# Linear attention and a feed-forward layer in one kernel: one batch's value loads behind a transpose, and another order of matmul products

## The chip, the cores and the metric

The kernel runs on one core of a Trainium2 chip. The core has a matrix engine (TensorE, shown as PE, its weight loads as PEld), a vector engine (VectorE, DVE), an activation engine (ScalarE, ACT), a general engine (GpSimd, POOL) and a queue engine that only issues transfers (SyncE, SP). Each takes its instructions in program order and waits on semaphores. Transfers are issued from SP, from POOL or from ACT and are carried out by 16 DMA engines that all of them share. TensorE reads from the on-chip memory SBUF and writes its results to eight PSUM banks[...].

The metric is the time of one execution on the device, in microseconds (us). Below about half a per cent a change of this kernel can't be told from none.

## The reference

There are 8 batches, 8 heads, 576 rows and 64 columns for each of q, k and v, in float32. The first part is attention with two separate softmaxes and no score matrix, the second a normalised feed-forward layer of width 2048 on 512 columns:

```python
q_s = softmax(q over the columns)          # per row
k_s = softmax(k over the rows)             # per column
kv  = einsum('bhsd,bhse->bhde', k_s, v)    # 64 x 64 per head
att = einsum('bhsd,bhde->bhse', q_s, kv)
x   = att with the heads side by side      # 8 x 576 x 512
xn  = (x - mean) / sqrt(var + 1e-6) * g_ln
out = x + relu(xn @ w_ch1) @ w_ch2
```

## The kernel before

**Tiling.** Each batch gives one chunk of 512 rows (chunks 0 to 7); the 64 rows left over in each of the 8 batches form a ninth chunk, called C9 in the code. A chunk's rows are held as four tiles t = 0 to 3 of 128 rows. All matrix work is in bfloat16.

**A chunk's attention.** `exp_q` and `exp_k` (ACT, lines 208 and 173) take the exponentials. `eq_T` (line 240) transposes the exponentials of q with one DMA from SP (line 236) into a tile `eqT`. `kv_mm` (line 275) multiplies k by v, with v taken from the tile `vm`; DVE scales the result into `kv_sb`. `po_mm` (line 313) multiplies `eqT` by `kv_sb`, and `x_fast` (line 372) turns the result into rows `x` and centred rows `xn`. `xn_T` (line 243) transposes `xn` by DMA into `xnT`, two tiles a time. For the ninth chunk, `x_rest` and `xn_out` stand in for `x_fast`.

**A chunk's feed-forward.** The first matmul, from chunk 2 on, is `mm1_fast` (line 581). It mixes plain column blocks (`plain m`), half blocks (`part`) and a Strassen-Winograd scheme with seven products P1 to P7 for each of two groups. The order of these pieces is a list of tokens in `plan`: `x` builds the differences of xnT (tile `ts`, line 561), `C` copies P1's bank as the start of P2 (ACT, line 605), `E` builds the start of P3 (DVE, line 639), `L` finishes one quarter (DVE, line 645). The second matmul, `mm2_fast` (line 804), uses seven products of 16 matmuls; line 722 issues them all and line 706 makes the sums `hs` that they need. For the ninth chunk it is `last_products` (line 753), in the order 1, 5, 2, 6, 7, 3, 4, and its rows leave in small stores on SP and ACT (line 773). There `seed_c` copies product 1's bank as the start of product 2, `copy_u("s2")` copies the bank after product 6 (line 748), and `seed_e` adds it to product 5's bank as the start of product 3.

**What sets the order.** Every engine's order is the program order. `run` (line 885) walks a chunk's matmul steps, each with a weight in units (a 128x512 matmul is one unit, half a one half), and before each step emits the side work whose due time in units has passed. A chunk is 60 units of first matmul and 56 of second. The side work of chunk c prepares chunks c+1 and c+2. All due times of chunks 2 to 7 stand in `plan`; those of chunk 1 stand in `second_side` (line 967).

**The loads in question.** `load_batch` (line 1157) loads q and k of a batch from SP and v in eight DMAs of 64 KB from POOL (line 1168); the DMA changes float32 to bfloat16 on the way and writes pieces of 64 columns into `vm`. In chunk 1's side work batch 3's q is loaded at unit 8, its k at unit 31 and its v at unit 40, while `eq_T(2)`, which chunk 2's attention needs within the same chunk, is due at unit 14.2. The outputs of each chunk go out from POOL (lines 494 and 740), so they are queued behind v's loads.

```python
s += [(10, lambda: exp_q(2, 0, 4)), (14, lambda: exp_q(2, 2, 4)), (14.2, lambda: eq_T(2))]
s += [(p, lambda w=w: load_batch(3, (w,))) for p, w in ((8, 2), (31, 0), (40, 1))]
```

The plan's entries that matter: `order` and `o9` are the token orders of chunks 2 to 7 and of the ninth; `xT` and `rT` place the transposes of xn; `prep` places exp_q, eq_T, the left-over rows and exp_k of the batch after next; `qw1` places four sums of the first weights, needed from chunk 2 on; `s9` places four sums of the ninth chunk; `rest` places the ninth chunk's attention in chunk 7.

Of the kernel before, what the change touches and what calls it, by code (L numbers as in the profile page):

```python
# [21 lines left out]
def kernel(  # L22
# [16 lines left out]
    nc = tc.nc  # L39
# [5 lines left out]
    T = 4  # L45
# [4 lines left out]
    NP = H // 2  # L50
# [6 lines left out]
    NG = 2  # L57
    M0 = KO2 - 4 * NG
    plan = dict(
        order=('P1 0|x 0|C 0|part 0|part 2|P2 0|P5 0|x 1|P6 0|E 0|plain 3|P7 0|plain 2|P3 0|P1 1|C 1|P4 0|L 0|plain 5|P6 1|P5 1|P2 1|plain 4|E 1|P7 1|plain 6|plain 7|P4 1|L 1|P3 1').split('|'),  # L60
        red=[9.5, 19.0, 21.0, 26.5, 35.5],
        kv=[6.0, 26.0],
        po=[[37.5, 42.5], [45.0, 48], [56, 67.5], [84.5, 90.0]],
        sq=[47, 62.5, 85.0, 109.0],
        xT=[58.0, 98.5, 110.5],
        prep=[62, 80.0, 92.5, 95.0, 97.5, 112.5],
        sum=60,
        qw1=[40, 53, 59.0, 79.0],
        o9=('x 0|x 1|P1 0|C 0|plain 3|part 0|P2 0|P6 0|plain 6|plain 4|P5 0|plain 2|plain 5|P7 0|part 2|P1 1|E 0|C 1|P4 0|L 0|P3 0|P5 1|P6 1|E 1|plain 7|P7 1|P3 1|L 1|P2 1|P4 1').split('|'),
        s9=[54.5, 58.0, 58.0, 58.5],  # L70
        rest=[[23.5, 28.0, 38.0, 51.0], [34.0, 50.5, 61.5, 65.0], [47.0, 63.0, 74.0, 80.0], [62.0, 87.0, 90.0, 92.0]],
        rT=[85.5, 115.0, 120.0],
    )
    T0 = 6
    P0 = S // T0
# [26 lines left out]
    gate = const.tile([P, 4], FP32)  # L102
# [68 lines left out]
    eks, eqs, eqTs, xs, xnTs, rstds = {}, {}, {}, {}, {}, {}  # L171
# [68 lines left out]
    def eq_T(c):  # L240
        dma_T(eqTs[c], eqs[c][0].rearrange("p t h d -> p (t h d)"), 0, T)
# [282 lines left out]
    def quarter_w2(i, g):  # L524

        ks = slice(4 * g, 4 * g + 4)
        rows = [w2_sb[:, 8 * g + odd : 8 * g + 8 : 2, :] for odd in range(2)]
        (b11, b12), (b21, b22) = [(r[:, :, 0:DH2], r[:, :, DH2:DM]) for r in rows]
        t1, t2, t3, t4 = [w2_q[:, n, ks, :] for n in range(4)]
        dst, x, y = ((t1, b12, b11), (t3, b22, b12), (t2, b22, t1), (t4, b21, t2))[i]  # L530
        nc.vector.tensor_sub(out=dst, in0=x, in1=y)
# [163 lines left out]
    def sum_h(g, i):  # L695

        if g == 0 and i == 0:
            hbox["s"] = mlp.tile([P, 4, KH, 2 * P], BF16, tag="hs", name="hs", bufs=1)
        ks = slice(KH // 2 * g, KH // 2 * g + KH // 2)
        s1, s2, s3, s4 = [hbox["s"][:, n, ks] for n in range(4)]  # L700
        a11, a12, a21, a22 = [h_part(odd, half, ks) for half in range(2) for odd in range(2)]
        dst, x, y, op = (
            (s1, a21, a22, ALU.add), (s2, s1, a11, ALU.subtract),
            (s3, a11, a21, ALU.subtract), (s4, a12, s2, ALU.subtract),
        )[i]
        nc.vector.tensor_tensor(out=dst, in0=x, in1=y, op=op)  # L706
# [18 lines left out]
    def bank(name):  # L725
        slot = {"a": 4, "c": 5, "b": 1, "e": 3, "d": 0}[name]
        hbox[name] = bank_of([P, 2, DH2], FP32, "b" + name, slot)
# [18 lines left out]
    def copy_u(name):  # L746
        hbox[name] = mlp.tile([P, 2, DH2], FP32, tag=name, name=name, bufs=1)
        nc.scalar.copy(hbox[name], hbox["a"])  # L748

    def add_u(dst, src):  # L750
        nc.vector.tensor_tensor(out=hbox[dst], in0=hbox["b"], in1=hbox[src], op=ALU.add)

    def last_products(product):

        c = C9
        yl = raw.tile([P, T, DM], FP32, tag="qt", name="yl")

        def part(t, col):
            return yl[:, t, DH2 * col : DH2 * col + DH2]

        def stt(t, col, src, add=None):
            cols = slice(DH2 * col, DH2 * col + DH2)
            nc.vector.scalar_tensor_tensor(
                part(t, col), in0=src, scalar=rstds[c][:, t : t + 1],
                in1=xs[c][0][:, t, cols] if add is None else add, op0=ALU.mult, op1=ALU.add,
            )

        def store(t0, tn, col):
            cols = slice(DH2 * col, DH2 * col + DH2)
            for half, eng in enumerate((nc.sync, nc.scalar)):  # L770
                ps = slice(64 * half, 64 * half + 64)
                to = out[2 * t0 + half : 2 * (t0 + tn) - 1 + half : 2, SM:S, cols]
                eng.dma_start(to.transpose([1, 0, 2]), yl[ps, t0 : t0 + tn, cols])

        def both(name, t0, col, add=False):
            for t in range(2):
                stt(t0 + t, col, hbox[name][:, t], part(t0 + t, col) if add else None)

        def own_bank():
            bank("d")  # L780

        def seed_e():
            bank("e")
            add_u("e", "s2")

        def seed_c():
            bank("c")
            nc.scalar.copy(hbox["c"], hbox["a"])

        product(1, "a", first=True, at={  # L790
            0: [lambda: sum_h(1, 0), lambda: sum_h(1, 1), lambda: sum_h(1, 2), lambda: sum_h(1, 3)],
            15: [seed_c]})
        product(5, "b", first=True)
        product(2, "c", at={15: [lambda: both("c", 0, 0), lambda: store(0, 2, 0)]})
        product(6, "a", at={15: [lambda: copy_u("s2"), seed_e]})
        product(7, "a", at={0: [lambda: both("b", 2, 1)], 15: [
            lambda: both("a", 2, 1, True), lambda: stt(3, 0, hbox["a"][:, 1]),
            lambda: store(2, 2, 1)]})
        product(3, "e", at={15: [lambda: both("e", 0, 1), lambda: store(0, 2, 1), own_bank]})
        product(4, "a", ts=(0,), at={7: [lambda: stt(2, 0, hbox["a"][:, 0]), lambda: store(2, 1, 0)]})  # L800
        product(4, "d", ts=(1,), own=True, at={
            15: [lambda: stt(3, 0, hbox["d"][:, 1], part(3, 0)), lambda: store(3, 1, 0)]})
# [164 lines left out]
    def second_side():  # L967

        s = [(p, lambda i=i: quarter_w2(i, 1)) for i, p in enumerate((1, 4, 44, 46))]
        s += [(8.0, lambda: xn_pT(1, 3, nc.scalar))]  # L970
        s += [(10, lambda: exp_q(2, 0, 4)), (14, lambda: exp_q(2, 2, 4)), (14.2, lambda: eq_T(2))]
        s += [(p, lambda i=i: quarter_w1(i)) for i, p in enumerate(plan["qw1"])]
        s += [(42, lambda: square_sum(1, 2)), (50, lambda: square_sum(1, 3)), (71, lambda: rstd_op(1))]
        s += [(p, lambda w=w: load_batch(3, (w,))) for p, w in ((8, 2), (31, 0), (40, 1))]
        s += [(100, lambda: load_batch(4, (2,)))]
        s += [(p + 15, fn) for p, fn in sums_fast(2)]
        s += [(18, lambda: exp_k(2, 0, 4)), (22, lambda: exp_k(2, 2, 4)), (26, lambda: prep_kvrem(2))]
        s += [
            (p, lambda j=j, e=e: cast_v(2, j, e))
            for p, j, e in ((31, 0, None), (31.4, 1, None), (31.8, 2, None), (32.2, 3, None))  # L980
        ]
        s += spread(
            [lambda j=j, t=t: kv_mm(2, j, t) for j in range(NP) for t in range(T + 1)], 43, 53
        )
        s += [(53, lambda: start_x(2))]
        for t, (p0, p1) in enumerate(((55, 58), (64, 67), (75, 80), (87, 93))):
            s += spread([lambda t=t, i=i: po_mm(2, t, i) for i in range(NP)], p0, p1)
            s += [(p1, lambda t=t: x_fast(2, t)), ((73, 82, 92, 105)[t], lambda t=t: square_sum(2, t))]
        s += [(78, lambda: xn_T(2, 0, 2)), (98, lambda: xn_T(2, 2, 2)), (106, lambda: rstd_op(2))]
        s += [(75, lambda: exp_q(3, 0, 4)), (79, lambda: exp_q(3, 2, 4)), (85, lambda: eq_T(3))]  # L990
        s += [(97, lambda: exp_k(3, 0, 4)), (108, lambda: exp_k(3, 2, 4)), (113, lambda: prep_kvrem(3))]
        return s
# [37 lines left out]
    def xn_pT(c, t, eng):  # L1030
        pe_T(xnTs[c], xs[c][2][:, t], t, eng)
# [125 lines left out]
    def load_batch(b, parts=(2, 0, 1)):  # L1157

        alloc(b, parts)
        for which in parts:  # L1160
            if which != 1:
                nc.vector.memset(raws[b][which][0:1, 0, 0, 0:1], 0.0)
        for which in parts:
            if which != 1:
                load_main(nc.sync, b, which, 0, H)
                continue
            for h in range(H):
                nc.gpsimd.dma_start(  # L1168
                    vm[:, b % 2, :, h // 2, 64 * (h % 2) : 64 * (h % 2) + 64],
                    v[b, h, 0:SM, :].rearrange("(p t) d -> p t d", t=T),  # L1170
                )
        if 1 in parts:
            load_kvrem(nc.sync, b)
# [114 lines left out]
```

## Time and profile before

Seven runs gave a median of 283.59 us, between 282.07 and 285.1. The profiled execution took 282.14 us, of which the profile's span is 280.4; 1.7 us lie outside the span.

| where | span, us | TensorE busy, us | VectorE busy, us | ScalarE busy, us |
|---|---|---|---|---|
| start to chunk 0's first matmuls | 0 to 34.0 | 32.54 | 19.59 | 22.09 |
| chunk 0's second matmul, chunk 1's first rows | 34.0 to 62.0 | 27.71 | 22.06 | 18.48 |
| rest of chunk 1 | 62.0 to 85.5 | 19.69 | 16.95 | 14.51 |
| chunk 2 | 85.5 to 112.7 | 27.20 | 22.64 | 21.11 |
| chunk 3 (4, 5 and 6 are alike) | 112.7 to 140.0 | 27.30 | 22.67 | 20.64 |
| chunk 7 | 221.9 to 249.0 | 27.10 | 23.96 | 18.63 |
| ninth chunk, with the last stores | 249.0 to 280.4 | 25.89 | 16.02 | 12.09 |

Each row is one stretch of the span. How to read it: an engine that is busy all the time can only be helped by fewer or faster instructions; one with gaps can be helped by whatever ends the gap. TensorE has its gaps in three places: the beginning, the rest of chunk 1, and the ninth chunk.

### The profile page before, as it was taken

The numbers are of one execution on the slowest core, as the hardware profiler recorded it, in microseconds if no ns is written. First come the engines' busy times: TensorE is split into PE (matmuls) and PEld (weight loads), VectorE is DVE, ScalarE is ACT, GpSimd is POOL, SyncE is SP. The second block draws the span as 40 slices with busy tenths as digits, with TensorE's granted clock in tenths as the row PEclk, the third lists the DMA queues.
The fourth block names the chain that finished last, engine by engine and source line by source line (L and its number), as shares of the span: only waits on it lengthen the run. The fifth ranks groups of instructions, "written<-read, shape, count | busy, mean of one in ns | idle before, by whom it ended". The sixth has DMA issues, their size and how long they took to land.

```text
span 280.4 us, 6073 instructions
## 1 busy us (share of the span) xinstructions
PE 269.3 (96%) x2362; PEld 214.2 (76%) x2365; DVE 213.0 (76%) x492; ACT 186.7 (67%) x365; POOL 66.8 (24%) x104
## 2 busy tenths in 40 slices
PE   8999999994999999999999999999999999999993
PEld 6888856762788688868986988698779877887673
DVE  4673778683988897889788978797879979982853
ACT  4568862793577888587868776877786489557500
POOL 3931224560007400820181018102000300030000
PEclk9999999999799999999999999999999999999999
DMA  7999999999489997799499948954920910160014
GB/s 189 243 207 206 335 212 331 230 243 214 76 148 297 247 204 111 227 233 168 89 288 232 128 105 264 127 86 106 244 42 8 204 57 0 37 182 9 2 37 112
DMA packets 84767, 45.41 MB, mean 162 GB/s; under 512 B 61442, under 2 KB 81410, under 8 KB 84739
## 3 DMA queue, kind: packets, MB, share of 16 engines
q0 software_dynamic: 32272, 22.09, 42.0%
q1 hardware_dynamic: 51874, 22.42, 38.7%
q10 hardware_dynamic: 592, 0.52, 0.6%
q8 instruction: 18, 0.29, 0.4%
q14 instruction: 11, 0.08, 0.1%
HBM read 36.70 MB, written 9.44 MB: 165 GB/s over the span
## 4 chain that ended last, share of the span: by engine, by line
PE 88%; DMA 4%; DVE 4%; ACT 2%; issue 0%; DVEq 0%
PE ba L722 19%; PE q L578 15%; PE ph L457 14%; PE ph L472 9%; PE bc L722 5%; PE be L722 5%; PE bb L722 5%; PE pc L517 4%; DMA eqT<-eq 4%; PE warm L903 3%; PE pkv L288 3%; PE po L322 3%; DVE hs L706 1%; PE ptr L1012 1%; ACT eq L212 1%; PE po L329 1%
## 5 line engine op out<-in xcount | busy, mean ns | idle before, releaser
L722 PEld LDWEIGHTS <-hs 128*128 128x128 bf16 x512 | 49.8, 98 | 7.2 <-issue 0.9
L457 PE MATMUL ph<-xnT,w_sb 128*128 128x512 bf16 x200 | 54.0, 385 | 0.0
L740 POOL DMA_DIRECT2D out_dram<-ot x28 | 15.2, 548 | 140.4 <-DVE ot L734 140.4
L447 ACT ACTIVATE hT<-ph 128x512 bf16<-128x512 f32 x50 | 29.9, 605 | 16.5 <-PE ph L457 15.4
L722 PEld LDWEIGHTS <-hT 128*128 128x128 bf16 x384 | 36.3, 99 | 4.7 <-ACT hT L598 0.3
L472 PE MATMUL ph<-xnT,w_sb 128*128 128x256 bf16 (+1 forms) x320 | 37.1, 267 | 0.0
L1168 POOL DMA_DIRECT2D vm<-in_v_dram x40 | 29.6, 745 | 11.1 <-DMA out_dram<-ot 6.1
L457 PEld LDWEIGHTS <-w_sb 128*128 128x128 bf16 x200 | 19.7, 99 | 15.9 <-issue 0.8
L472 PEld LDWEIGHTS <-w_sb 128*128 128x128 bf16 x320 | 29.1, 98 | 3.1
L722 PE MATMUL ba<-w_q,hs 128*128 128x256 bf16 x256 | 30.7, 273 | 0.7 <-ACT s L748 0.7
L322 PE MATMUL po<-kv_sb,eqT 128*128 128x128 bf16 x128 | 24.3, 222 | 4.0 <-DMA eqT<-eq 3.8
L375 DVE SCALAR_TENSOR_TENSOR x<-po,rq 128x512 bf16<-128x512 f32 x30 | 20.6, 686 | 9.2 <-PE po L322 9.0
L598 ACT ACTIVATE hT<-q 128x512 bf16<-128x512 f32 x42 | 24.1, 597 | 2.8 <-PE q L578 2.6
L228 DVE TENSOR_REDUCE zq<-eq 128x8 f32<-128x512 bf16 x32 | 20.9, 680 | 6.2 <-ACT eq L212 3.5
L578 PE MATMUL q<-ts,w_q 128*128 128x256 bf16 x168 | 25.7, 273 | 0.0
L482 ACT ACTIVATE hT<-ph 128x512 bf16<-128x512 f32 x34 | 20.3, 601 | 7.3 <-PE ph L472 7.1
L578 PEld LDWEIGHTS <-w_q 128*128 128x128 bf16 x224 | 19.8, 98 | 6.1 <-issue 0.3
L706 DVE TENSOR_TENSOR hs<-hT 128x1024 bf16<-128x1024 bf16 x32 | 21.3, 688 | 3.2 <-ACT hT L447 1.6
L748 ACT COPY s<-ba 128x512 f32<-128x512 f32 x15 | 8.8, 585 | 20.7 <-PE ba L722 20.6
L288 PE MATMUL pkv<-vm,ek 128*128 128x129 bf16 x112 | 21.2, 220 | 0.0
L650 ACT COPY s<-q 128x512 f32<-128x512 f32 x28 | 16.3, 582 | 2.5 <-PE q L578 2.4
L322 PEld LDWEIGHTS <-eqT 128*128 128x128 bf16 x128 | 11.9, 99 | 7.8 <-DMA eqT<-eq 4.3
(145 smaller groups left out, 509.0 us busy)
## 6 DMA issues: line engine op xcount, KB each, us to landing
out_dram<-ot POOLq DMA_DIRECT2D x32, 256.0 KB, 3.7
qt<-in_q_dram SPq DMA_DIRECT2D x5, 1024.0 KB, 10.9
kt<-in_k_dram SPq DMA_DIRECT2D x5, 1024.0 KB, 9.0
w_sb<-in_moe_w_ch_dram POOLq DMA_DIRECT2D x8, 512.0 KB, 14.2
vm<-in_v_dram POOLq DMA_DIRECT2D x40, 64.0 KB, 9.2
qt<-in_q_dram POOLq DMA_DIRECT2D x2, 1024.0 KB, 15.8
kt<-in_k_dram POOLq DMA_DIRECT2D x2, 1024.0 KB, 16.2
kt<-in_k_dram SPq DMA_DIRECT2D x4, 288.0 KB, 5.8
```

The source lines that it names most:

```text
L228: nc.vector.reduce_sum(eqs[c][1][:, t], eqs[c][0][:, t], axis=AX.X)
L288: nc.tensor.matmul(pkv[:, j % 2, 0:w], lhsT, rhs, start=(t == 0 and j % 2 == 0), stop=(t == last), skip_group_check=True,)
L322: nc.tensor.matmul(pobox["p"][:, i * P : i * P + P], eqTs[c][:, t, i, :], kv_sb[:, c, i, :], start=True, stop=True,)
L375: nc.vector.scalar_tensor_tensor(x[:, t].rearrange("p (h d) -> p h d", h=H), in0=pobox[c, t].rearrange("p (h d) -> p h d", h=H), scalar=1. ...
L447: nc.scalar.activation(dst, src, AF.Relu)
L457: nc.tensor.matmul(hbox["ph"], w1_sb[:, ko, m * P : (m + 1) * P], xnTs[c][:, :, ko, :], start=(ko == 0), stop=(ko == KO1 - 1),)
L472: nc.tensor.matmul(ph[:, m % 2, at : at + tn], w1_sb[:, ko, m * P : (m + 1) * P], xnTs[c][:, t0 : t0 + tn, ko, :], start=(m % 2 == 0 and a ...
L578: nc.tensor.matmul(hbox["q", slot][:, m], lhsT, rhs, start=first and i == 0, stop=ko == 1, skip_group_check=True)
L598: nc.scalar.activation(hbox["h"][:, m0 : m0 + 2, 2 * nh : 2 * nh + 2], hbox["q", slot].rearrange("p m (t c) -> p m t c", t=2), AF.Relu,)
L706: nc.vector.tensor_tensor(out=dst, in0=x, in1=y, op=op)
L722: nc.tensor.matmul(hbox[bank][:, t], lhsT, rhs, start=first and (own or t == 0) and k == 0, stop=k == KH - 1, skip_group_check=True)
L1168: nc.gpsimd.dma_start(vm[:, b % 2, :, h // 2, 64 * (h % 2) : 64 * (h % 2) + 64], v[b, h, 0:SM, :].rearrange("(p t) d -> p t d", t=T),)
```

## The change

It holds batch 3's v loads: POOL first copies a few values of `eqT` of batch 2, so everything behind that copy on POOL waits until that transpose has landed. It changes the token orders of the first matmul, moves due times of side work in chunks 1 to 7, and in the ninth chunk's second matmul puts product 6 ahead of product 2, with product 5's rows taken out at product 2's first step. The computation is the same; one small copy on POOL is added.

```diff
-        order=('P1 0|x 0|C 0|part 0|part 2|P2 0|P5 0|x 1|P6 0|E 0|plain 3|P7 0|plain 2|P3 0|P1 1|C 1|P4 0|L 0|plain 5|P6 1|P5 1|P2 1|plain 4|E 1|P7 1|plain 6|plain 7|P4 1|L 1|P3 1').split('|'),
+        order=('x 0|P1 0|C 0|part 0|P2 0|part 2|P5 0|x 1|P6 0|E 0|plain 3|P7 0|plain 2|L 0|P3 0|P1 1|C 1|P4 0|plain 5|P6 1|plain 4|P5 1|P2 1|P7 1|E 1|plain 7|plain 6|L 1|P4 1|P3 1').split('|'),
-        xT=[58.0, 98.5, 110.5],
-        prep=[62, 80.0, 92.5, 95.0, 97.5, 112.5],
+        xT=[60.5, 123.5, 110.5],
+        prep=[68, 71.0, 86.0, 90.5, 101.5, 113.5],
-        qw1=[40, 53, 59.0, 79.0],
-        o9=('x 0|x 1|P1 0|C 0|plain 3|part 0|P2 0|P6 0|plain 6|plain 4|P5 0|plain 2|plain 5|P7 0|part 2|P1 1|E 0|C 1|P4 0|L 0|P3 0|P5 1|P6 1|E 1|plain 7|P7 1|P3 1|L 1|P2 1|P4 1').split('|'),
-        s9=[54.5, 58.0, 58.0, 58.5],
-        rest=[[23.5, 28.0, 38.0, 51.0], [34.0, 50.5, 61.5, 65.0], [47.0, 63.0, 74.0, 80.0], [62.0, 87.0, 90.0, 92.0]],
-        rT=[85.5, 115.0, 120.0],
+        qw1=[47.5, 51.5, 55.0, 63.0],
+        o9=('P1 0|C 0|plain 5|plain 4|P2 0|x 0|plain 2|plain 3|part 0|P6 0|part 2|P5 0|x 1|P7 0|E 0|P1 1|C 1|plain 6|P3 0|plain 7|L 0|P6 1|P4 0|P5 1|E 1|P7 1|P2 1|L 1|P4 1|P3 1').split('|'),
+        s9=[47, 52.5, 52.5, 57.5],
+        rest=[[12.5, 29.5, 39.5, 49.5], [27.5, 35.5, 64.5, 73.0], [45.5, 60.0, 72.5, 73.5], [61.5, 67.0, 73.5, 91.0]],
+        rT=[83.5, 129.5, 91.0],
...
-        product(2, "c", at={15: [lambda: both("c", 0, 0), lambda: store(0, 2, 0)]})
         product(6, "a", at={15: [lambda: copy_u("s2"), seed_e]})
-        product(7, "a", at={0: [lambda: both("b", 2, 1)], 15: [
+        product(2, "c", at={0: [lambda: both("b", 2, 1)], 15: [lambda: both("c", 0, 0), lambda: store(0, 2, 0)]})
+        product(7, "a", at={15: [
...
-        s += [(p, lambda w=w: load_batch(3, (w,))) for p, w in ((8, 2), (31, 0), (40, 1))]
+        s += [(p, lambda w=w: load_batch(3, (w,))) for p, w in ((8, 2), (31, 0))]
+        s += [(40, lambda: (nc.gpsimd.tensor_copy(out=gate, in_=eqTs[2][:, T - 1, NP - 1, 0:4]), load_batch(3, (1,))))]
```

## The prediction

> **What bounds the kernel now.** I read the page's first lines, then TensorE's waits, then the stretches around the longest wait.
>
> ```profile
> PE 269.3 (96%) x2362; PEld 214.2 (76%) x2365; DVE 213.0 (76%) x492; ACT 186.7 (67%) x365; POOL 66.8 (24%) x104
> PEclk9999999999799999999999999999999999999999
> PE po L322 <- DMA eqT<-eq: 3.8, 1, 3.8
> PE ba L722 <- ACT s L748: 0.7, 1, 0.7
> PE bb L722 <- DVE hs L706: 0.3, 1, 0.3
> ```
>
> TensorE is busy for 269.3 of 280.4 us, so 11.1 us of gaps are all there is to win, besides time at a lower clock. Its waits, from the list of who waited for whom, are few. One is large: 3.8 us for batch 2's transposed q. In the second row a digit is a fortieth of the span, 7 us; its single 7 falls at 70 to 77 us, just behind that wait. Table of stretches of 1 us there (PE, PEld, DVE, ACT, POOL busy, then granted clock, DMA share, GB/s):
>
> ```profile
> 63.00:64.00 1.00, 1.00 (x12) 0.63 (x9) 0.76 (x4) 1.00 (x3) 0.00 (x0) 1.00 1.65 137
> 66.00:67.00 1.00, 0.00 (x0) 0.00 (x0) 0.00 (x0) 0.00 (x0) 0.00 (x0) 1.00 2.50 147
> 69.00:70.00 1.00, 1.00 (x9) 0.43 (x6) 0.36 (x1) 0.60 (x1) 0.00 (x0) 0.88 1.10 345
> 70.00:71.00 1.00, 1.00 (x4) 0.43 (x3) 0.89 (x4) 0.60 (x1) 0.00 (x0) 0.50 1.18 307
> 71.00:72.00 1.00, 1.00 (x5) 0.41 (x3) 1.00 (x2) 0.07 (x1) 0.00 (x0) 0.50 1.26 164
> 72.00:73.00 1.00, 1.00 (x7) 0.81 (x6) 0.45 (x2) 0.97 (x3) 0.00 (x0) 0.50 0.09 17
> ```
>
> At 66 every engine stands still while the DMA engines are full. Then TensorE runs again, at half clock for 3 us. The timeline of the transfers says why the transpose is late:
>
> ```profile
> 53.83 0.39 SPq L146 DMA_DIRECT2D qt<-in_q_dram  x1
> 54.57 5.31 POOL L1168 DMA_DIRECT2D vm<-in_v_dram  x7
> 56.72 5.41 SPq L236 DMA_TRANSPOSE eqT<-eq  x1
> 68.56 0.23 PE L322 MATMUL po<-kv_sb,eqT 128*128 128x128 bf16 x1 [3.81 <-DMA eqT<-eq]
> DMA to landing us min/median/max: 4.3/5.1/11.8
> ```
>
> The last line is of all seven transposes of q: this one is the 11.8, others take 4.3 to 5.2. It shares the DMA engines with 1 MB of batch 3's q, issued 2.9 us before it, and with v's eight transfers. From 85.5 to 249.0 TensorE has no gap at all:
>
> ```profile
> 112.70:140.00 27.30, 27.30 (x246) 22.38 (x244) 22.67 (x54) 20.64 (x40) 8.10 (x13) 1.00 0.98 184
> ```
>
> **The change, part by part.**
>
> *v held behind the transpose.* TensorE runs out of other work at 68.56 - 3.81 = 64.75. Without v the transpose should take what the others take: 56.72 + 5.2 = 61.9, 2.8 us early. But q's 1 MB stays ahead of it on SP. The Trainium skill (DMA: Bandwidth & Descriptors, section Queues, rings and completion order) speaks against the change: each DMA engine consumes one queue's descriptors in ring order, and goes round-robin only between queues. Holding POOL's queue thus gives SP's a larger share, but does not let the transpose past q. In the trace q landed 8.3 us after issue, at 62.1; the shortest of the later q loads took 6.4, which would be 60.2. By the rule, in full order, 60.2 + 5.1 = 65.3, so 0.6 us of waiting remain; with q as late as now, 62.1 + 5.1 = 67.2, or 2.5 us. By the row, 61.9 and none. I take the row: the transposes' time includes about 3 us of issue, which can run while q drains. Ends: 0 and 2.5 us left.
>
> With the wait goes its clock loss: 3 us at 0.50 and the edges (0.88 in the row at 69, 0.71 mean from 72 to 74) lose 3 x 0.5 + 0.12 + 0.08 = 1.7 us. What of a remainder? The skill (TensorE: Matmul & The Clock Gate, Part 1: The HAM clock gate) lets the clock fall only after an idle window of about 3.4 us; by it a remainder of 2.5 us costs no clock. In proportion to the trace's one such gap it would cost 2.5/3.8 x 1.7 = 1.1. The 3.8 us row fits the rule and I take 0, with 1.1 for the range. **Gain 3.8 + 1.7 = 5.5 us.**
>
> What is late next? POOL's eight v issues now start at about 62.5 instead of 54.6 and take 8 x 0.745 = 6.0, to 68.5; landing was 8.4 to 11.4 us, so the last arrives by 80. Their user is chunk 2's `kv_mm`: first at unit 6, last head pair at unit 21 of a chunk that will start at 85.5 - 5.5 = 80.0, so at about 81.4 (whose v was issued first, landed by 74) to 85. Behind them on POOL stand chunk 1's outputs, due at 84.54 - 5.5 = 79. The copy itself is some 0.2 us of POOL (the same copy at 5.42). Left-over k and v rows are on SP and don't wait for POOL. k of batch 3, on SP behind the transpose's issue, may go earlier by some 2 us.
>
> The cost that is new: v now runs beside the next transposes, which had empty DMA engines (share 0.04 and 0.00 from 72 to 76). They are issued 5.5 us sooner, at 70.0 (xn, first half), 72.2 (q of batch 3) and 75.6 (xn, second half). A half transpose took 3.1 us alone and 8.1 at 98.6 beside v and q loads: 70.0 + 8.1 = 78.1, before 80.0. The second half: alone 78.8; if q's transpose ahead of it takes 9 us, 81.2 + 3.2 = 84.4, against its first use in a matmul at 81.8. Ends 0 and 2.6; I take 0, as v's bytes are through by about 74.
>
> *Weight sums (qw1).* Four DVE sums of 0.69 us, needed only from chunk 2, move within chunk 1: two of them now stand among the kv scalings at 63 to 65, where DVE was 0.76 to 0.96 busy. Some 0.3 us of delay for `kv_sb` at most, and the matmul that needs it comes half a us later. 0, up to 0.3.
>
> *Chunks 2 to 7 (order, xT, prep).* No TensorE gap is there to win; it can only be lost. The nearest edge: P2 moves ahead of `part 2`, so it follows P1 by 8 half matmuls (0.87 us) instead of 16. It needs ACT's copy of P1's bank:
>
> ```profile
> 113.04 1.04 PE L472 MATMUL ph<-xnT,w_sb 128*128 128x256 bf16 x8
> 113.24 0.57 ACT L605 COPY q<-q 128x512 f32<-128x512 f32 x1 [1.12 <-PE q L578]
> 113.97 0.38 PE L472 MATMUL ph<-xnT,w_sb 128*128 128x256 bf16 x2
> ```
>
> The copy ends at 113.81, and P2 would start at 113.97: 0.16 us to spare. ACT reaches it in time: 1.12 us idle ahead of it now, and though one exp_k (1.05 us) now runs after product 7's copy instead of before it, ACT's rows from 109.31 on (0.48 copy, 0.76 square, 0.53 root, twice 0.95 to 1.05 exp_k) then end at 113.0 to 113.2, just before P1 ends. Cost 0, or 0.15 in each of 6 chunks = 0.9. The second transpose of xn keeps its place on SP, which issues nothing between units 98.5 and 123.5; the loads' markers on DVE go behind the first differences, 0.8 us later for transfers used 20 us later. The q transpose moves from unit 92.5 to 86, to 20 us before use. L 0 earlier and E 1 later: P3 keeps 1.3 us between E 1's emission and use. 0.
>
> *Chunk 7 (rest).* `po_mm` starts at unit 12.5, 2.9 us in, at 224.8 in old times; its q transpose, issued at 215.91 plus 5.2, lands at 221.1. DVE has the same operations from 236 to 245.5, all full; ACT's copy after product 6 now queues behind the last squares and ends some 0.15 us before product 7. 0, up to 0.3 lost.
>
> *Ninth chunk.* Product 7 waited 0.68 us (0.7 in the waits) for ACT's 0.59 us copy of product 6's bank. Now product 2 (16 matmuls, 1.75 us) stands between: all gone, 0.7. Product 2's own start was copied during product 5 already. The 0.34 us wait of product 5 for its fifth sum: DVE ended it at 264.93. By my count of the new o9 and s9 DVE does two of the earlier sums ahead of its last L, and ends the fifth at about 264.65: 0.3 gone. The end, from product 4 through two stores, is unchanged. **Gain 1.0**, between 0.4 and 1.1.
>
> Sum: 282.1 - 5.5 - 1.0 = 275.6 in the profiled execution's terms. Its time is 1.5 us below the median of the seven, 283.6. If that spread has nothing to do with the stall, the new median is 277.1; if it is the stall that varies with the transfers, 275.6. I take 276.3.
>
> **Rivals.**
>
> *A part of the wait stays or moves.* The transpose stays behind q (2.5 left, perhaps 1.1 of clock), or chunk 2's start waits for its rows (2.6). For: ring order, and DMA shares above 1 there. Against: 4.3 to 5.2 us for all other q transposes. 276.3 + 2.5 = 278.8, up to 279.9.
>
> *The hold frees nothing,* because q and the transpose alone fill the time: landing again near 68.5. Only the ninth chunk's 1.0 and perhaps the half us of shorter queueing remain: 282.1. For: the transpose's issue itself took 5.41 us on SP. Against: other issues of it take 1.5 to 3.1.
>
> *Slower: P2 waits for ACT in every chunk.* Place: the copy at line 605, chunks 2 to 7. To eat 6.5 us it must be 1.1 us late in each beyond the 0.16 to spare, that is when exp_k, moved behind product 7, waits for k or pushes ACT 1.2 us past P1's end. It decides from there; at 1.5 us late in each, 1.35 x 6 = 8.1 and 276.3 + 8.1 = 284.4. Against: k has been there for 10 us by then.
>
> **How the numbers follow.** Stall gone, all else hidden: 0.74, from 274.9 to 277.9. A part stays: 0.16. Frees nothing: 0.06. Slower: 0.04. The range goes from 274.9 to 279.3, which takes in the first and most of the second. A measurement of this kernel tells 0.5% (1.4 us) from no change; faster is the first two, 0.90; the third is the same, 0.06; slower 0.04.
>
> **What would show it.** Right: no wait of line 322 for eqT above 0.6 us, no clock digit below 9 after the start, the longest q transpose near 5 to 8 us, v's issues starting after 61, chunks of 27.3 us each, and no wait of line 722 for ACT. Wrong: idle TensorE at line 578 behind ACT, at the head of chunk 2, or at line 322 again.

## The result, and the profile after

The changed kernel takes 275.52 us in the median of 12 runs (274.95 to 278.0), the kernel before 283.59 in 31 runs (281.94 to 286.73). The ratio is 0.9738, with a 95% interval of 0.9712 to 0.9764: faster by 2.6%. It is not the ratio of the two medians, since it leaves out the kernel before's three longest runs, each more than 1.5% above its fastest. The profiled execution took 275.08 us with a span of 273.3, against 282.14 and 280.4; the span shrank by 7.1.

From the page of after: span, busy times with shares, and the clock in fortieths of the span.

```profile
span 273.3 us, 6069 instructions
...
PE 266.8 (98%) x2362; PEld 213.7 (78%) x2365; DVE 212.2 (78%) x492; ACT 187.3 (69%) x365; POOL 67.0 (25%) x105
...
PEclk9999999999999999999999999999999999999999
```

TensorE has as many matmuls as before. Its gaps fell from 11.1 us (280.4 - 269.3) to 6.5 (273.3 - 266.8); the other 2.5 us of the 7.1 are matmul time, and most of that is the clock: no digit is a 7 any more. TensorE's waits after (us in all, how often, longest):

```profile
PE warm L903 <- DVE junk L1066: 1.1, 1, 1.1
PE q L578 <- ACT s L650: 0.2, 1, 0.2
PE ptr L1013 <- DVE xn L368: 0.2, 1, 0.2
PE ph L472 <- ACT xnT L1134: 0.2, 1, 0.2
PE po L322 <- DVE kv_sb L297: 0.2, 1, 0.2
```

The wait of 3.8 us for `eqT`, the 0.7 for ACT's `s` and the 0.3 for `hs` are gone. Two of 0.2 us are new: that of line 578, in the ninth chunk, and that of line 472, at the start. The timeline of after round the old wait (start, us, engine, line; the idle time before an instruction and its releaser in brackets):

```profile
53.75 0.39 SPq L146 DMA_DIRECT2D qt<-in_q_dram  x1
56.64 5.40 SPq L236 DMA_TRANSPOSE eqT<-eq  x1
62.22 0.44 SPq L146 DMA_DIRECT2D kt<-in_k_dram  x1
...
64.14 0.19 POOL L975 CAST gate<-eqT 128x4 f32<-128x4 bf16 x1 [9.62 <-DMA eqT<-eq]
64.67 6.04 POOL L1169 DMA_DIRECT2D vm<-in_v_dram  x8 [0.35 <-issue]
...
64.51 0.22 PE L322 MATMUL po<-kv_sb,eqT 128*128 128x128 bf16 x1
```

The copy on POOL starts at 64.14, when the transpose has landed: at 64.04, 7.4 us after its issue at 56.64, where it was 11.8. TensorE loads the result as weights at 64.30 and multiplies with it at 64.51, so less than half a us was to spare. The stretch of chunk 3 and one of 2 us behind the old gap, from the table of stretches (PE, PEld, DVE, ACT, POOL busy, granted clock, DMA share, GB/s):

```profile
107.20:134.50 27.30, 27.30 (x247) 22.40 (x245) 22.59 (x54) 20.72 (x41) 8.09 (x13) 1.00 1.17 184
66.00:68.00 2.00, 2.00 (x19) 1.44 (x17) 1.89 (x5) 1.61 (x4) 1.88 (x4) 1.00 1.38 306
```

In chunk 3's stretch TensorE is busy throughout, as before, and the clock behind the transpose is full. To say where 7.1 us went, I cut every trace at the same five instructions. A runs to the first `po_mm` matmul; B from there to the first `po_mm` matmul on batch 2's transposed q (the wait is in it); C to chunk 2's first product (the clock loss is in it); D, chunks 2 to 7, to the ninth chunk's first product; E to the start of VectorE's last operation. The rest of the span is 4.2 to 4.4 us everywhere.

| kernel | A | B | C | D | E | span |
|---|---|---|---|---|---|---|
| before | 14.64 | 53.92 | 16.75 | 163.48 | 27.30 | 280.4 |
| after | 14.41 | 50.10 | 15.14 | 163.48 | 25.89 | 273.3 |
| before minus after | 0.23 | 3.82 | 1.61 | 0.00 | 1.41 | 7.1 |

So the wait brought 3.8, the clock behind it 1.6, chunks 2 to 7 nothing, and the ninth chunk 1.4 in this profile (1.3 in the mean of seven, as shown below).

### The profile page after: what moved, and what is told of

Same layout as the page of the kernel before. It is cut to its first block, busy times and chain, and to the rows that moved or that the text cites. A ratio compares the mean times of both kernels' runs of the same rounds, so it can differ in the third digit from the quotient of the medians.

```text
span 273.3 us, 6069 instructions
## 1 busy us (share of the span) xinstructions
PE 266.8 (98%) x2362; PEld 213.7 (78%) x2365; DVE 212.2 (78%) x492; ACT 187.3 (69%) x365; POOL 67.0 (25%) x105
## 4 chain that ended last, share of the span: by engine, by line
PE 95%; DVE 2%; ACT 0%; issue 0%; DVEq 0%
PE ba L722 20%; PE ph L457 16%; PE q L578 16%; PE ph L472 11%; PE bb L722 5%; PE bc L722 5%; PE be L722 5%; PE pc L517 4%; PE warm L903 4%; PE pkv L288 3%; PE po L322 3%; PE ptr L1013 1%; PE po L329 1%; DVE xn L368 1%; DVE x L375 1%; DVE kv_sb L297 0%
## 5 line engine op out<-in xcount | busy, mean ns | idle before, releaser
L457 PE MATMUL ph<-xnT,w_sb 128*128 128x512 bf16 x200 | 53.0, 379 | 0.0
L472 PE MATMUL ph<-xnT,w_sb 128*128 128x256 bf16 (+1 forms) x320 | 37.8, 267 | 0.2 <-ACT xnT L1134 0.2
L472 PEld LDWEIGHTS <-w_sb 128*128 128x128 bf16 x320 | 29.1, 98 | 3.5 <-DMA w_sb<-in_moe_w_ch_dram 0.4
L457 PEld LDWEIGHTS <-w_sb 128*128 128x128 bf16 x200 | 19.2, 98 | 15.6 <-issue 0.2
L578 PEld LDWEIGHTS <-w_sb 128*128 128x128 bf16 x168 | 15.6, 98 | 2.9 <-issue 0.4
```

What stands on the lines that cost most here:

```text
L457: nc.tensor.matmul(hbox["ph"], w1_sb[:, ko, m * P : (m + 1) * P], xnTs[c][:, :, ko, :], start=(ko == 0), stop=(ko == KO1 - 1),)
L472: nc.tensor.matmul(ph[:, m % 2, at : at + tn], w1_sb[:, ko, m * P : (m + 1) * P], xnTs[c][:, t0 : t0 + tn, ko, :], start=(m % 2 == 0 and a ...
L578: nc.tensor.matmul(hbox["q", slot][:, m], lhsT, rhs, start=first and i == 0, stop=ko == 1, skip_group_check=True)
```

## The experiments

No kernel here leaves out or changes a part of the computation; two add matmuls whose result nobody reads. A stage letter stands for its time in the kernel's profiled execution. Medians are of 6 runs, or 12 where said. Ratios are to the kernel before on the same chip, with 95% intervals. Where an experiment moves one stage, the stage times of its trace decide, since the total also carries the spread told of in the last section.

### The hold: alone, and everything but it

`e1_hold_only` is the kernel before with the two lines of the hold and nothing else.

```diff
-        s += [(p, lambda w=w: load_batch(3, (w,))) for p, w in ((8, 2), (31, 0), (40, 1))]
+        s += [(p, lambda w=w: load_batch(3, (w,))) for p, w in ((8, 2), (31, 0))]
+        s += [(40, lambda: (nc.gpsimd.tensor_copy(out=gate, in_=eqTs[2][:, T - 1, NP - 1, 0:4]), load_batch(3, (1,))))]
```

> The kernel before with only the hold of batch 3's v. If the hold carries the stall's 5.5 us: ratio about 0.980, chunk 1's wait for eqT below 0.6 us, ninth chunk as before with its waits of 0.7 and 0.3 us. If the shifted side work of chunk 1 (the weight sums) were needed as well, the wait would stay above 1 us and the ratio above 0.985.

Measured: 279.28 us, ratio 0.9817 (0.9773 to 0.9861). B is 49.89 and C 15.14, so wait and clock loss are gone; D is 163.48 and E 27.30, as before. The profiled time, 279.08, is higher than these stages say because its A is 17.21: TensorE ran at half clock from 14 to 17 us, which other kernels show as well (last section). Five of its six runs have a mean clock of 0.993 or less; the sixth, at 0.999, took 276.50.

`e2_no_hold` is the changed kernel with the old line of loads.

```diff
-        s += [(p, lambda w=w: load_batch(3, (w,))) for p, w in ((8, 2), (31, 0))]
-        s += [(40, lambda: (nc.gpsimd.tensor_copy(out=gate, in_=eqTs[2][:, T - 1, NP - 1, 0:4]), load_batch(3, (1,))))]
+        s += [(p, lambda w=w: load_batch(3, (w,))) for p, w in ((8, 2), (31, 0), (40, 1))]
```

> The changed kernel without the hold, all else kept. If the hold alone removes the stall: the wait for eqT is back at about 3.8 us with half clock behind it, and only the ninth chunk's 1.4 us remain, ratio about 0.995. If the moves of side work did it, the ratio stays below 0.985.

Measured: 281.82 us in 12 runs, ratio 0.9932 (0.9903 to 0.9961). Its first wait of TensorE:

```profile
PE po L322 <- DMA eqT<-eq: 4.3, 1, 4.3
```

B is 54.46 and C 16.76, so wait and clock loss are both back; E stays at 26.13. The hold is what removes B's and C's part, and the rest of the change is what removes E's.

### Which neighbour delays the transpose

Two readings of the late transpose stood against each other: the DMA engines are shared, so v's bytes take its share; or SP's own queue is served in order, so q's 1 MB in front of it must be through first. `e6_q_behind_only` is the kernel before with batch 3's q issued behind the transpose, and v not held.

```diff
-        s += [(p, lambda w=w: load_batch(3, (w,))) for p, w in ((8, 2), (31, 0), (40, 1))]
+        s += [(p, lambda w=w: load_batch(3, (w,))) for p, w in ((14.3, 2), (31, 0), (40, 1))]
```

> The kernel before, v not held, but batch 3's q load put behind the q transpose on SP. If v's packets are what slows the transpose (shared engines): it still lands 9 us or more after issue, the wait stays above 2 us, ratio above 0.985. If q's 1 MB ahead on the same queue is the cost (ring order): it lands about 5 to 7 us after issue, the wait is gone, ratio about 0.980.

Measured: 276.87 us, ratio 0.9765 (0.9724 to 0.9806). From the timeline of `e6_q_behind_only`, SP and POOL, and the landing time of this transpose:

```profile
56.76 3.37 SPq L236 DMA_TRANSPOSE eqT<-eq  x1
60.23 0.52 SPq L146 DMA_DIRECT2D qt<-in_q_dram  x1
...
54.47 6.05 POOL L1168 DMA_DIRECT2D vm<-in_v_dram  x8
```
```profile
DMA to landing us min/median/max: 7.3/7.3/7.3
```

With v beside it as before, but q behind it, the transpose lands after 7.3 us, at 64.06: no wait, B 49.95, C 15.14. One neighbour out of the way is enough, whichever it is.

`e9_q_instead` is the changed kernel with that way in place of the hold (first diff), and `e3_both_behind` has both (second).

```diff
-        s += [(p, lambda w=w: load_batch(3, (w,))) for p, w in ((8, 2), (31, 0))]
-        s += [(40, lambda: (nc.gpsimd.tensor_copy(out=gate, in_=eqTs[2][:, T - 1, NP - 1, 0:4]), load_batch(3, (1,))))]
+        s += [(p, lambda w=w: load_batch(3, (w,))) for p, w in ((14.3, 2), (31, 0), (40, 1))]
```
```diff
-        s += [(p, lambda w=w: load_batch(3, (w,))) for p, w in ((8, 2), (31, 0))]
+        s += [(p, lambda w=w: load_batch(3, (w,))) for p, w in ((14.3, 2), (31, 0))]
```

> The changed kernel with v not held and batch 3's q put behind the transpose instead. If either transfer out of the way is enough: no wait for eqT, ratio 0.973 as the changed kernel. If the later k and q beside v delay the batch's exponentials: a wait in chunk 2, ratio above 0.98.

> The changed kernel with batch 3's q also put behind the q transpose on SP. If the transpose in the changed kernel is still held up by q on its own queue (it landed 7.4 us after issue): it lands 4.3 to 5.2 us after issue. TensorE had no wait there any more, so the time should stay the same, ratio about 0.973; if some executions of the changed kernel still stall there, the spread of its runs narrows.

Measured: `e9_q_instead` 276.67 us, ratio 0.9803 (0.9758 to 0.9848), transpose 6.6 us; `e3_both_behind` 276.4, ratio 0.9786 (0.9742 to 0.983), and this transpose, from `e3_both_behind`:

```profile
DMA to landing us min/median/max: 4.4/4.4/4.4
```

Neither has the wait, and neither is faster than the changed kernel: once the transpose is in time, more margin buys nothing. All profiled runs together give this transpose's time by what was beside it:

| beside the transpose | kernels | us to landing | us behind q's landing |
|---|---|---|---|
| q ahead, v running | before, e2, e5, e11 | 11.7 to 12.3 | 5.7 to 7.0 |
| q ahead, v held | after, e1, e4, e7, e8, e10, a1 | 5.4 to 7.4 | 1.6 to 1.9 |
| q behind, v running | e6, e9 | 6.6 to 7.3 | |
| q behind, v held | e3 | 4.4 | |

Against the 4.4 of the one profile with neither, each neighbour alone adds up to 3 us; both add over 7, more than the sum. The last column says more: the transpose never landed ahead of a q that stood before it on SP. With v held it came in a nearly constant time behind q, and the range of 5.4 to 7.4 us is that of q's own landing (6.5 to 8.7 us after issue). With v running it came 4 to 5 us later behind q. In after, from its view of the tile `qt`:

```profile
DMA to landing us min/median/max: 8.7/8.7/8.7
```

So q landed at 53.75 + 8.7 = 62.45, and the transpose at 64.04. In the kernel before q took 8.3, so in these two profiles the hold did not bring q in sooner. v's eight loads gained as well: held, they land in after in 3.8 to 6.7 us instead of 8.4 to 11.4.

### The clock loss: the gap, or the work behind it

`e5_filler` puts 36 matmuls whose result nobody reads into the old gap of the kernel before, `e11_half_filler` 18 of them (`warm(18)`), as a step of chunk 1's side work.

```diff
-        s += [(53, lambda: start_x(2))]
+        s += [(53, lambda: start_x(2)), (54.9, lambda: warm(36))]
```

> The kernel before with 36 idle matmuls (3.9 us of work whose result nobody reads) put on TensorE just ahead of the first matmul that waits for batch 2's transposed q. The stall's time stays filled, but TensorE isn't idle: if half clock after the gap is what costs the other 1.7 us, no clock digit falls there and the time is 1.7 us shorter than before, ratio 0.994. If the clock loss is covered by other waits: 1.000.

> The kernel before with 18 idle matmuls (1.95 us, nobody reads them) ahead of the first matmul that waits for batch 2's transposed q, so that about 1.9 us of idle wait remain. If a remainder of 2 us costs no clock (what the prediction took): no half clock behind it, and from that matmul to chunk 2's first product 15.1 us, as in the changed kernel, not 16.75 as before; about 1.6 us shorter than before. If the loss is in proportion to the gap: 15.9 us.

Measured: `e5_filler` 282.27 us in 12 runs, ratio 0.9994 (0.9963 to 1.0025); `e11_half_filler` 282.57 in 12 runs, ratio 0.9967 (0.9935 to 1.0). By time `e5_filler` missed the 0.994 that was expected if the half clock behind the gap is what costs; it came out at the 1.000 of the other reading. The traces say why. `e5_filler`, timeline of TensorE, and then one stretch behind the filler:

```profile
67.04 4.09 PE L903 MATMUL warm<-junk 128*128 128x256 bf16 x36
71.31 0.23 PE L322 MATMUL po<-kv_sb,eqT 128*128 128x128 bf16 x1 [0.17 <-DMA eqT<-eq]
```
```profile
72.00:73.00 1.00, 1.00 (x8) 0.46 (x6) 0.61 (x1) 0.57 (x2) 0.00 (x0) 1.00 1.12 355
```

B is 54.15, so the result is as late as ever, but the clock is 1.00 behind it and C is 15.07 instead of 16.75. In this profile the 1.7 us of C were the gap's doing, not that of the transfers or of the work behind it. It has the start's half clock too (A 17.16), so its span of 281.5 hides the gain. The other runs point the same way: 6 of its 12 have a mean clock of 0.996 or more, against 2 of the 51 of the kernel before in these experiments. But four of these six took 0.7 to 1.3 us more than usual outside the span, and that is not explained. The two of the kernel before, at 1.0 and 0.999, took 280.31 and 280.39 us; so, as far as mean clocks tell, its gap doesn't cost the clock in every execution. `e11_half_filler` leaves less than half of the gap:

```profile
68.79 0.23 PE L322 MATMUL po<-kv_sb,eqT 128*128 128x128 bf16 x1 [1.73 <-DMA eqT<-eq]
```
```profile
70.00:71.00 1.00, 1.00 (x7) 0.43 (x5) 0.89 (x4) 0.60 (x1) 0.00 (x0) 1.00 1.13 327
71.00:72.00 1.00, 1.00 (x13) 0.92 (x12) 1.00 (x3) 0.81 (x3) 0.00 (x0) 1.00 1.36 219
```

In this execution a gap of 1.73 us cost its own length and no clock (C 15.07; its D is 0.44 longer, with a wait of 0.3 for `xnT` at chunk 2). But only 2 of the kernel's 12 runs, this one among them, show a mean clock of 0.997 or more. A single trace doesn't tell where the others lost it, so whether a short gap always spares the clock is open.

### The ninth chunk: the swap and the sums

`e4_swap_undone` is the changed kernel with products 6 and 2 in their old order; `e8_o9_old` is the changed kernel with the ninth chunk's old token order and old sums, keeping the swap (the diff shows `s9`; `o9` goes back to the old list in the same way).

```diff
+        product(2, "c", at={15: [lambda: both("c", 0, 0), lambda: store(0, 2, 0)]})
         product(6, "a", at={15: [lambda: copy_u("s2"), seed_e]})
-        product(2, "c", at={0: [lambda: both("b", 2, 1)], 15: [lambda: both("c", 0, 0), lambda: store(0, 2, 0)]})
-        product(7, "a", at={15: [
+        product(7, "a", at={0: [lambda: both("b", 2, 1)], 15: [
```
```diff
...
-        s9=[47, 52.5, 52.5, 57.5],
...
+        s9=[54.5, 58.0, 58.0, 58.5],
```

> The changed kernel with the ninth chunk's products in the old order 1, 5, 2, 6, 7, 3, 4. If the swap is worth the wait it removes: 0.7 to 0.85 us longer than the changed kernel, a wait of about 0.7 us of line 722 for ACT's copy, ratio about 0.977. If the wait had been hidden by the end's stores anyway: no difference, 0.974.

> The changed kernel with the ninth chunk's old token order and old places of its four sums; the product swap stays. From the ninth chunk's first product to VectorE's last operation the kernel before takes 27.30 us, the changed one 25.89, and the changed one with the swap undone 26.88. If order and swap add up: 0.3 to 0.45 us longer than the changed kernel here, about 26.3, with a wait of about 0.3 us of line 722 for the sums. If the swap alone carried all of it: 25.9.

Measured: `e4_swap_undone` 276.28 us, ratio 0.9757 (0.9707 to 0.9807), E 26.88; `e8_o9_old` 276.07, ratio 0.9734 (0.9698 to 0.9771), E 26.53. The ratios don't show either part. E does: in the seven profiles with the changed ninth chunk (after, e2, e3, e7, e9, e10, a1) it is 25.89 to 26.13, mean 26.01, and after's is the shortest; in the five with the old one (before, e1, e5, e6, e11) it is 27.3. Against the mean, the swap undone costs 0.87 us, and the old order and sums 0.52, each a little more than expected. The same products on TensorE's timeline, first in `e4_swap_undone`, then in after:

```profile
262.32 1.91 PE L722 MATMUL ba<-w_q,hs 128*128 128x256 bf16 x16
264.91 1.91 PE L722 MATMUL ba<-w_q,hs 128*128 128x256 bf16 x16 [0.68 <-ACT s L748]
```
```profile
260.09 1.91 PE L722 MATMUL ba<-w_q,hs 128*128 128x256 bf16 x16
261.84 1.91 PE L722 MATMUL bc<-w_sb,hT 128*128 128x256 bf16 x16
263.58 1.91 PE L722 MATMUL ba<-w_q,hs 128*128 128x256 bf16 x16
```

From start to start, product 6 to product 7 takes 2.59 us in the old order, and 1.75 per product in the new one. So the swap is worth 0.84, though the wait reads 0.68: in the records products that follow without a wait overlap by 0.16 us (1.91 long, 1.75 apart), and a wait takes that overlap too. `e8_o9_old` keeps the other loss, that of the sums:

```profile
257.77 2.12 PE L722 MATMUL ba<-w_sb,hT 128*128 128x256 bf16 x16
259.73 0.60 PE L722 MATMUL bb<-w_q,hs 128*128 128x256 bf16 x4
260.67 1.48 PE L722 MATMUL bb<-w_q,hs 128*128 128x256 bf16 x12 [0.34 <-DVE hs L706]
261.99 1.91 PE L722 MATMUL ba<-w_q,hs 128*128 128x256 bf16 x16
```

Product 1 takes 1.96 from start to start and product 5 2.26, instead of 1.75 each: 0.7 together. The new order gives a little back at a matmul that waits for ACT in the first half of the chunk, again from after's timeline:

```profile
255.71 0.60 PE L578 MATMUL q<-ts,w_sb 128*128 128x256 bf16 x4 [0.24 <-ACT s L650]
```

The swap's 0.84 stands against 0.87 in E, and the order's 0.7 - 0.24 = 0.46 against 0.52. Together they are 1.3, and so is E's part by the mean: 27.3 - 26.01. After's 1.41 is 0.1 more, within the 0.24 by which E differs among the seven.

### The moved side work of chunks 1 to 7

`e7_side_old` is the changed kernel with the old `order`, `xT`, `prep`, `qw1`, `rest` and `rT`; the last of these and `qw1` are shown.

```diff
...
-        qw1=[47.5, 51.5, 55.0, 63.0],
+        qw1=[40, 53, 59.0, 79.0],
...
-        rT=[83.5, 129.5, 91.0],
+        rT=[85.5, 115.0, 120.0],
```

> The changed kernel with the old token order of chunks 2 to 7, old transposes, side work, weight sums and chunk 7's attention; hold, ninth chunk's order, its sums and products stay as changed. If these moves cost and bring nothing: the same as the changed kernel, ratio 0.973, chunks of 27.3 us. If the earlier attention of chunk 7 was needed: a TensorE wait near the ninth chunk's start, 0.3 to 1 us.

Measured: 275.62 us, ratio 0.9761 (0.9726 to 0.9795), with B 49.95, C 15.13, D 163.48, E 25.91. All these moves together are worth nothing that can be measured.

### The start, and the changed kernel again

`e10_gcp_late` is the changed kernel with eight one-row matmuls of the start (and the copy of their result) issued later, to see whether they bring on the half clock at 14 to 17 us. `a1_changed` is the changed kernel again.

```diff
-        gcp = bank_of([P, KO1], FP32, "gcp")
-        for ko in range(KO1):
...
-        nc.vector.tensor_copy(out=g_col, in_=gcp)
...
         eq_pT(0, 2, nc.vector)
+        gcp = bank_of([P, KO1], FP32, "gcp")
+        for ko in range(KO1):
...
+        nc.vector.tensor_copy(out=g_col, in_=gcp)
```

> The changed kernel with the eight 1-row matmuls that lay out g_ln in columns (line 1108, 0.94 us) moved from ahead of the first kv matmuls to behind the transposes of batch 0's third tile. Some executions run at half clock from 14 to 17 us, which costs 2.5 us. If the low use of TensorE by these matmuls, the one-row product before them and the one-column sums behind them sets that off: fewer executions with a mean clock below 0.995, and the start 0.5 to 0.9 us shorter. If other things bound the start: first attention product of batch 0 at 14.4 us as before, the same spread, ratio as the changed kernel.

> The changed kernel again, beside these three on the same chip: ratio about 0.974, a third of its executions 1 to 2.5 us longer by the clock at the start.

Measured: `e10_gcp_late` 276.28 us, ratio 0.9736 (0.97 to 0.9772); A is 13.94, 0.5 to 0.7 shorter, B 50.83, 0.7 longer, so the time comes back. None of its 6 runs had a mean clock under 0.995, against 3 of 6 of `a1_changed` and 4 of 12 of after: too few to call it a cure. `a1_changed` took 276.06 us, ratio 0.9757 (0.9705 to 0.9808), span 273.6, with the stages of after but for 0.2 in A, B and E. No version tried is faster than the changed kernel beyond the intervals.

## Why the prediction was right

The time (276.3 forecast, 275.52 measured) and the sum for the profiled execution (275.6 and 275.08) agree, and so do most steps. The landing of the transpose and the ninth chunk were mis-sized.

- **The wait:** 3.8 us forecast, 3.82 measured in B; `e1_hold_only` and `e2_no_hold` show that it is the hold. The landing inside it was mis-sized. I took 61.9, by the time of the other transposes, as if it could pass q; none of those had a megabyte of q just ahead, and in no profile with q ahead did this one land before q. The order of landing agrees with the ring-order rule of the Trainium skill (DMA: Bandwidth & Descriptors, section Queues, rings and completion order), which I had set aside; my sum by it, 65.3, was off by 1.3 because two sizes in it were wrong: q took 8.7 us, not 6.4, and the transpose came 1.6 us behind q, not 5.1. That its issue runs while q drains, the reason I gave, may explain the 1.6, but it never passed q. Of the 2.8 us to spare that I counted on, less than half a us was left: that nothing of the wait remained was luck in part.
- **The cause:** I blamed v's bytes, with q as the objection. Both are causes, and either one out of the way does it (`e6_q_behind_only`). q's part is its place ahead: the transpose lands behind it. v's part is what comes after q's landing, 1.6 to 1.9 us with v held and 5.7 to 7.0 with v running. Why v costs 4 to 5 us there, but at most 3 where q is not ahead, is open.
- **The clock:** 1.7 forecast, 1.61 measured in C, and the trace of `e5_filler` shows that it hung on the gap. On a remainder, the skill's idle window (TensorE: Matmul & The Clock Gate, Part 1: The HAM clock gate) fits the one trace of a 1.73 us gap: 0 lost, where proportion would give 1.73/3.8 x 1.7 = 0.8. As a rule that the clock falls only after some 3.4 us of idle time it is not what the traces show: the clock fell after 3.41 us with 2.2 of them idle, and at the start with none idle (last section).
- **v behind the transpose:** forecast at 62.5 to 68.5 on POOL, it was 64.67 to 70.71. It landed sooner after its issue than I took (3.8 to 6.7 us, not 8.4 to 11.4). No transpose behind it was late: those of xn took 3.2 to 3.6 us, and chunk 2 started without a wait. 0 was right.
- **Weight sums, chunks 2 to 7, chunk 7:** 0 forecast; D is 163.48 in both, and `e7_side_old` equals the changed kernel. The edge of 0.16 us at P2 never turned into a wait.
- **Ninth chunk:** 1.0 forecast, 1.41 measured (1.3 by the mean of seven), past my range of 0.4 to 1.1. I priced each wait at its entry in the list, 0.68 and 0.3. From start to start they were 0.84 and, with product 1's thinner overlap, 0.7; the new wait of 0.24 I had not foreseen.
- **From profile to median:** the median fell by 8.07, the profiled time by 7.06. I took the middle of two readings, 277.1 (the spread has nothing to do with the stall) and 275.6 (it has); the second was nearer. Among the 17 runs of before beside `e2_no_hold`, 14 had a mean clock of 0.990 or less, where the profiled one had 0.994; none of after's 12 is below 0.992. So the typical run of before lost more clock than the profiled one. Behind the stall or at the start, the runs without a trace don't tell.

## What to carry to other kernels

When a transfer is late, list what shares the DMA engines with it and what stands ahead of it on its own queue. Count its landing from that of the transfer ahead of it, not from its own issue. Moving one of the two was enough here; moving both gave more margin and no time. Price a TensorE wait from start to start of the groups around it, with the clock in the rows behind it added: here 3.8 us of waiting cost 5.4 in the profiled execution, and 0.68 cost 0.84. Where an engine has no gap, moving its neighbours' work brings nothing.

## What the runs showed of the hardware

The granted clock also fell where TensorE had no gap. In five of the fourteen profiles, of kernels with and without the hold, it was 0.50 for 3.4 us from about 14 us on; the start is the same code in all but `e10_gcp_late`. A stretch of `e3_both_behind`, and the same stretch of before:

```profile
14.00:15.00 1.00, 1.00 (x13) 1.00 (x11) 0.10 (x1) 0.00 (x0) 0.85 (x1) 0.50 1.15 207
```
```profile
14.00:15.00 1.00, 1.00 (x15) 0.90 (x13) 0.68 (x3) 0.61 (x1) 0.05 (x1) 1.00 1.29 222
```

TensorE is busy for the whole stretch in both, and was from 8 to 14 us in both. In `e1_hold_only`, `e3_both_behind` and `e5_filler` the half clock begins at 13.5 to 13.8 us and lengthens A (17.05 to 17.21, otherwise 13.9 to 15.3); in `e8_o9_old` and `e9_q_instead` it begins at 14.2 to 14.3. A and B together are 66.9 and 67.1 in `e1_hold_only` and `e3_both_behind`, 65.8 in the last two, and 64.5 to 65.2 in the six profiles with neither this nor the stall. So it costs 1.7 to 2.6 us, or 0.6 to 1.3 where it begins later. The runs of the changed kernel lie 3 us apart, and its longer ones have a mean clock of 0.992 to 0.994, where these five profiles have 0.991 to 0.994; that is why stage times decided above.

The clock records of the traces show what sets these five executions apart. In all fourteen, the clock changed only at whole multiples of 3.41 us from its first record, and that record lies anywhere from 4.0 to 7.0 us. Ahead of the end of the span, every stretch at half clock lasted one such step. Counted this way, a step begins between 10.0 and 10.9 us in exactly the five profiles with the half clock at the start, which follows with the next step; in the nine others a step begins between 11.0 and 12.4. What runs there is TensorE's thinnest work, matmuls of one row or one column between 10 and 13.7 us. That this work brings the half clock on is not shown: `e10_gcp_late` moved eight of these matmuls, but its one profile has a step that begins at 11.5, as others have that lost nothing.

The gap fits the same steps. In before TensorE was idle for 2.2 us of the step from 66.35 to 69.76, in `e2_no_hold` for 2.6 of its step there, and the next step ran at half clock. In `e5_filler` 3.0 us of the wait fall into the step from 68.3 to 71.7, but the filler was busy in it, and the clock stayed full. In `e11_half_filler` the whole gap of 1.73 us fell into one step, and the next ran at full clock. By these four traces a gap's cost in clock depends on how much of it falls into one step, and so differs between executions of one program. Where the limit lies is open.
